# Causal gate taps as zero-padded 128-row matmuls, with a new order table

## The chip, the cores and the metric

One core of a Trainium2 chip. The metric is device time in microseconds; the kernel before took 230.55 us (median of three runs, 229.36 to 231.44).

## The reference

Two layers in a row: a linear attention with exponential features, and a gated unit with a causal convolution of five taps. Cut to what matters:

```python
# q, k, v: [8, 8, 576, 64] (batch, heads, sequence, head size); w_phi: [64, 128]
def phi(x):
    proj = x @ w_phi
    proj = proj - max(abs(proj), axis=-1)
    return concat(exp(proj), exp(-proj))              # 256 features
kv  = einsum('bhsf,bhsd->bhfd', phi(k), v)
den = phi(q) . sum_s(phi(k)) + 1e-6
x   = (phi(q) . kv) / den                             # [8, 576, 512], heads side by side

gate_pre[:, s] = sum over t of conv_w[t] * x[:, s + t - 4]   # five taps, zeros before the start
gate = sigmoid(gate_pre)
out  = (gate * (x @ w_val)) @ w_out                   # float32, [8, 576, 512]
```

## The kernel before

The eight batches are a software pipeline. Each batch goes through the same stages, and several batches are in work at once:

- **Loads.** Batch 0's k and q come as float32 on SP's queue (L506, L504) and are transposed on TensorE (`tp32`, L514). Later batches' q and k come through GpSimd's queue with a cast (`load`, L528); batch 1 is transposed on TensorE (`tp16`, L533, tasks `xk1.0` to `xk1.2` and `xq1.*`, copied out by `tc16`, L538 or L540), batches 2 to 7 by DMA transposes on SP's queue (`xpose`, L543). v comes on SP's queue (L509). A few one-element copies on GpSimd (`hold`, `holdx`, L488 and L491) make the loads behind them wait.
- **Features.** 18 column blocks of 128 rows per batch, in five units of 4, 4, 4, 4 and 2. For each unit: a projection (`kp`, `qm`, L555), the absolute maximum on VectorE (L562), and two exponentials on ScalarE, of the plus and of the minus sign (`kexp`, L572; `qexp`, L657 and L660). For q the maximum is subtracted in a second projection (`qp`, L642 and L649) that needs the maxima of all units (`mqt`, L631, and `mqr`, L634).
- **State.** `ek` (L581) makes scale factors from k's maxima, `vs` (L588, L589) scales v by them on GpSimd, into VT, in two groups of two; `st` (L598) multiplies features and scaled v, and `kv` (L606 or L610) copies the result out.
- **Attention out.** `num` (L670, L677), normalization on VectorE (`nrm`, L688 and L691), transposes (`xtp`, L699 and L703), copies (L711, L716) into the tile XT, and `halo` on GpSimd (L720, L721), which puts the last positions of one half ahead of the other.
- **Gate and out.** XT holds even positions in partitions 0 to 63 and odd ones in 64 to 127, 288 of each. A tap is a product with a diagonal matrix of the tap's weights. Where a pair of taps fills both halves, one 128-row matmul does two taps (GF, L732, eight per gate task). The fifth tap of each parity touches one half only: a 64x64 quarter of the array with the matrix GQ (L739, four per gate task). Four gate tasks per batch; then `tanh` (L743), `val` (L751), the product (`gv`, L757), `out` (L775), copies to OUTS (L608, L612) and stores (L797, L803). `c_gt` (L472, L475, L477) builds GF and GQ once, on GpSimd.

TensorE works in shapes, which the rows give as rows*columns: 128*128, 64*128 (projections, `st`, `val`), 128*64 (L732 and L677) and 64*64 (L739).

Nothing is scheduled by the compiler. `build` lists the tasks; the table `ORDER` gives their order, written out by hand as numbers, and each engine and each queue gets its instructions in that order and runs them in order. `FLEX` says which engine does the tasks that may go to two, `BANKS` which of the eight PSUM banks each group uses. `WARM` and the tasks `warm` add matmuls on a tile of ones (L481), whose result nobody reads.

Of the kernel before, what the change touches and what calls it, by code (L numbers as in the profile page):

```python
# [28 lines left out]
NW = 14  # L29
# [5 lines left out]
    "8:7:5 21:7:1 214:5:1 "  # L35
# [6 lines left out]
    "15 16 18 17 20 19 22 21 24 35 23 37 26 25 36 39 57 27 38 59 41 32 34 170 40 43 61 60 33 172 55 42 73 74 64 47 171 174 58 "  # L42
    "193 311 49 63 44 0 28 76 62 56 50 29 48 65 93 75 45 94 67 53 91 66 54 30 46 92 51 68 97 173 31 89 98 77 188 90 184 52 "
    "185 95 194 96 69 186 189 72 79 5 187 99 228 2 71 100 229 104 313 190 105 70 226 80 9 106 227 101 78 1 103 234 191 110 "
    "175 235 192 10 111 230 178 102 182 179 183 107 112 231 180 108 195 312 11 181 232 109 84 233 81 197 203 82 206 196 6 85 "
    "113 83 314 204 198 8 7 114 199 12 201 319 236 237 205 86 200 320 115 238 202 207 87 210 4 88 116 239 208 315 14 240 118 "
    "117 316 209 211 119 122 212 128 317 241 129 215 242 123 217 124 318 214 125 120 130 213 176 131 243 321 216 329 121 13 "
    "332 3 322 126 331 177 127 132 218 324 330 354 433 434 219 323 355 247 221 248 435 139 220 352 140 353 250 141 436 252 "
    "358 359 149 222 251 249 325 437 150 133 327 356 134 357 244 438 135 246 360 361 223 326 245 333 224 439 136 225 328 137 "
    "265 335 362 266 142 138 363 334 337 143 145 144 338 336 151 339 367 152 440 369 146 253 340 370 254 441 368 267 268 255 "  # L50
    "341 259 442 372 269 256 261 343 260 364 371 443 262 147 366 444 342 148 450 365 446 447 263 452 154 449 445 451 166 155 "
    "257 264 562 448 563 258 458 565 167 344 459 453 347 485 564 345 461 273 346 274 486 454 460 348 455 270 275 477 478 162 "
    "456 271 566 481 457 158 482 163 479 272 480 376 159 349 377 160 483 284 484 378 156 462 350 161 464 285 373 465 351 157 "
    "276 374 567 463 277 487 286 466 488 568 375 467 279 278 492 569 287 379 493 280 153 380 288 281 468 570 494 282 289 164 "
    "573 283 571 577 575 391 472 578 295 576 299 392 165 296 574 393 572 579 290 469 685 686 394 300 606 470 580 607 395 381 "
    "688 471 495 687 382 385 473 496 307 386 497 608 308 581 383 583 609 387 303 584 388 489 304 384 689 291 491 582 389 490 "
    "292 498 604 390 499 474 605 475 500 585 476 610 588 405 611 399 406 690 400 586 410 407 401 691 396 587 411 501 397 612 "
    "503 414 692 613 398 502 589 402 415 591 614 403 693 408 590 404 615 293 592 616 409 593 297 510 618 595 301 506 511 168 "
    "412 617 507 294 696 413 622 298 699 729 812 813 516 730 302 624 425 416 169 594 517 504 623 814 426 421 698 505 518 619 "
    "422 519 815 508 621 697 599 512 429 620 513 727 816 430 509 628 596 629 520 431 728 731 600 630 597 694 625 732 598 735 "  # L60
    "432 627 514 736 417 626 515 712 733 418 695 715 601 734 714 700 602 702 713 521 603 524 703 522 817 527 523 701 525 528 "
    "530 526 818 529 531 704 532 737 705 708 819 537 711 738 707 539 538 820 709 535 706 305 540 633 710 427 536 739 423 716 "
    "533 634 309 740 722 306 631 534 741 748 428 632 856 750 745 424 935 857 541 643 746 635 936 310 644 639 723 747 636 542 "
    "937 640 749 751 645 637 646 753 938 558 543 638 647 752 823 559 717 854 862 641 826 863 939 546 855 825 724 718 642 547 "
    "860 725 861 554 726 824 742 555 858 744 719 859 827 720 743 828 940 651 721 648 941 652 649 662 653 650 754 829 419 663 "
    "654 548 755 830 831 556 655 832 756 942 420 656 766 549 864 833 767 760 757 557 550 834 865 943 835 761 821 768 837 660 "
    "544 769 560 551 758 770 661 838 869 759 657 870 836 822 664 944 871 866 665 658 868 762 666 763 659 867 872 545 667 979 "
    "873 839 980 764 561 677 842 945 765 874 673 678 840 981 674 780 982 843 675 771 841 850 781 679 772 985 782 774 986 552 "
    "676 773 977 775 978 950 680 776 777 844 953 954 553 778 955 785 779 952 669 786 668 951 783 845 670 956 671 789 784 957 "
    "875 672 790 849 983 877 846 984 946 847 876 787 848 949 878 788 851 880 947 962 791 879 852 965 804 853 948 963 958 987 "  # L70
    "805 883 959 964 796 988 966 884 881 960 972 893 882 887 797 894 889 961 885 888 992 973 989 994 886 890 798 895 800 896 "
    "991 891 799 808 801 993 897 968 892 974 967 990 1001 975 1002 998 976 681 1003 809 999 969 682 810 995 1000 970 907 996 "
    "971 904 908 997 905 792 811 909 1004 906 1006 1005 793 1012 1007 1010 1016 1013 1008 916 1011 898 1009 1017 1014 901 917 "
    "1018 899 902 1019 910 1015 903 794 900 1020 806 914 683 911 795 912 802 807 1024 913 684 1021 915 803 1025 1027 1026 "
    "1030 1028 1031 1022 1029 923 1032 1037 924 1023 925 1033 1039 926 1034 1035 1040 1038 927 919 928 1036 931 929 920 1041 "
    "1054 932 918 921 930 1046 933 1055 922 1058 1056 1047 934 1042 1048 1059 1062 1057 1060 1050 1043 1049 1051 1044 1063 "
    "1052 1061 1045 1053 "
)
FLEX = (
    "ADAADAAAAAPPAPPDAAAADDAADAPPDPPDDAAADPPDPPDDADAPPAPPDAAAAAPPAPPDAADDPPAPPAAADADPPDPPDDADAPDDPPADDDDA"  # L80
)
BANKS = (
    "460006544445500124166757234523230145452301456767723672301674501445674652345230145234501276045505450101236723016701016767"
    "674230145670101011236736601674501014523236503323016723674501454567232370123456723450124567741230123236745236732374567452"
    "323450123452367010016767230167676452322367450167016767453636623674567452301452301454500101010101232320101732014501676767"
    "010122154523230145674545676767454450145674545450012303223672301010145236636423236745456701010145014524523670167452323457"
    "201230145450123457466234567014567230123674545701672301672345230177674501234545016744555"
# [69 lines left out]
def build(plan, em=None):  # L157
# [16 lines left out]

    for i in range(NW):
        A("warm", 0, i, "PE", 0.44, fn("warm2"), [], plan.group("warm", 1), 0)

    for b in range(B):
# [144 lines left out]
        for j in range(4):  # L323
            g = plan.group("gate", 2)
            ga = A("gate", b, j, "PE", 0.52, fn("gate", b, j, 0), xall, g, 2)
            gt = h["gate", b, j] = A("gate", b, j, "PE", 0.14, fn("gate", b, j, 1), [ga], g, 7, rank=-1)
            h["tanh", b, j] = A("tanh", b, j, "ACT", act(576), fn("tanh", b, j), [gt, G("gv", b - 1, j)], g)
# [25 lines left out]
class Emit:  # L353
    def __init__(self, nc, tc, ctx, q, k, v, w_phi, moe_w_val, moe_conv_w, moe_w_out, out):
# [63 lines left out]
        self.GQ = T("GQ", [P, H, D])  # L418
# [3 lines left out]
        for i in range(2):  # L422
            nc.gpsimd.memset(self.MQP[i][:, :], 0.0)
            nc.gpsimd.memset(self.XT[i][:, :, :, 0:HALO], 0.0)
# [41 lines left out]
    def c_gt(self, t):  # L466
        nc = self.nc

        for c, taps in ((0, (2, 3, 0, 1, 4)), (1, (3, 4, 1, 2, 0))):
            r = slice(c * D, (c + 1) * D)  # L470
            for i, tap in enumerate(taps):
                nc.gpsimd.tensor_copy(self.SC[r, :, i:i + 1], self.cwP[r, :, tap:tap + 1])  # L472
        with nc.allow_low_precision("bf16 taps"):
            for i in range(4):
                nc.gpsimd.tensor_tensor(self.GF[:, :, i, :], self.SC[:, :, i:i + 1].to_broadcast([P, H, D]),  # L475
                                        self.ID2[:, :].unsqueeze(1).to_broadcast([P, H, D]), ALU.mult)
            nc.gpsimd.tensor_tensor(self.GQ[:, :, :], self.SC[:, :, 4:5].to_broadcast([P, H, D]),  # L477
                                    self.ID2[:, :].unsqueeze(1).to_broadcast([P, H, D]), ALU.mult)
# [3 lines left out]

    def warm2(self, t):
        for _ in range(2):
            self.warm(t.grp.banks[0])
# [238 lines left out]
    def gate(self, t, b, j, part):  # L724
# [9 lines left out]
        else:  # L734
            for par, s, c in ((0, 0, 0), (1, 2, 1)):
                for h2 in range(2):
                    h = 2 * j + h2
                    rows = slice(c * D, (c + 1) * D)
                    self.nc.tensor.matmul(self.PS[h2 * D:(h2 + 1) * D, t.grp.banks[par], 0:R], self.GQ[rows, h, :],  # L739
                                          X[rows, h, :, HALO - 8 * s:HALO - 8 * s + XH], start=False, stop=True)  # L740
# [121 lines left out]
```

## Time and the profile before

| | |
|---|---|
| time, three runs | 230.55 us (229.36 to 231.44) |
| span of the profiled execution | 233.1 us |
| last matmul of the profiled execution | starts 225.76, busy 1.89 us for the last eight |
| TensorE busy | 211.9 us (91%), 4027 matmuls |
| ScalarE busy | 181.7 us (78%) |
| VectorE busy | 176.4 us (76%) |
| GpSimd busy | 103.0 us (44%) |
| DMA | 39.87 MB, mean 171 GB/s |

The profile is one execution, and matmuls are pipelined, so a busy TensorE is not a TensorE at its peak: the distance between the starts of two groups of matmuls tells more than their busy time. In a timeline row the first number is the start in us from the span's start, the second the busy time; a row ends with the number of instructions (x8) and, in brackets, the idle time before it and what ended it. In the chain of work that ended last, the columns are start, share of time in us, and what. In a row of windows, the columns are the window, its length, busy time of PE, PEld, DVE, ACT and POOL, the granted TensorE clock, the DMA share and GB/s.

### The profile page before, as it was taken

The page shows a single profiled execution, that of the slowest core. Times are in us where ns is not written, and L with a number is a line of the kernel's source. Part 1 is how long each engine was busy: PE and PEld are TensorE (multiplying, and loading weights), DVE is VectorE, ACT ScalarE, POOL GpSimd, SP SyncE. Part 2 cuts the span into 40 slices and gives each one's busy share as a digit, 9 for nine tenths or more (in the row PEclk, how much of TensorE's full clock was granted, in tenths as well). Part 3 has the DMA queues.
Part 4 walks back from the last instruction along what each step waited for, and adds up shares of the span by engine and source line. Part 5 has one row for each costly group of instructions (what it writes and reads, how often), then busy time and mean ns, then how long its engine had stood idle before and what let it go on. Part 6 is the DMA issues. An engine that isn't in the chain of part 4 may idle for free.

```text
span 233.1 us, 9168 instructions
## 1 busy us (share of the span) xinstructions
PE 211.9 (91%) x4027; PEld 145.5 (62%) x4027; DVE 176.4 (76%) x264; ACT 181.7 (78%) x267; POOL 103.0 (44%) x158
## 2 busy tenths in 40 slices
PE   7888997699998999999998599999999999999990
PEld 3566555567676576666766367676665867676640
DVE  2569776998789877998899549796888899583361
ACT  2878999799899987998898479978998999913320
POOL 2715992694059329800495006940009739100020
PEclk9999999999999999999999979999999999999999
DMA  6999935999699779968999981969984106156156
GB/s 199 338 257 272 208 55 160 209 181 174 116 207 242 127 160 178 302 114 114 229 167 296 167 232 30 148 126 229 263 277 143 52 3 139 37 83 204 45 177 184
DMA packets 49426, 39.87 MB, mean 171 GB/s; under 512 B 33706, under 2 KB 38826, under 8 KB 49322
## 3 DMA queue, kind: packets, MB, share of 16 engines
q1 hardware_dynamic: 43136, 29.63, 52.4%
q0 software_dynamic: 5760, 9.31, 23.8%
q8 instruction: 31, 0.51, 0.8%
q10 hardware_dynamic: 490, 0.35, 0.5%
q14 instruction: 9, 0.07, 0.1%
HBM read 30.49 MB, written 9.44 MB: 171 GB/s over the span
## 4 chain that ended last, share of the span: by engine, by line
PE 59%; DVE 16%; DMA 6%; POOL 5%; issue 5%; ACT 4%; ACTq 1%; SPq 1%; DVEq 0%
PE PS L751 12%; PE PS L775 10%; PE PS L732 7%; PE PS L555 7%; PE PS L598 6%; DVE MK L562 4%; DMA kT<-KQN 4%; DVE XN L691 4%; PE PS L670 3%; DVE MQP L562 3%; PE PS L739 3%; POOL VT L588 3%; PE PS L642 3%; DMA KTIL<-in_k_dram 2%; DVE GV L757 2%
## 5 line engine op out<-in xcount | busy, mean ns | idle before, releaser
L588 POOL TENSOR_TENSOR VT<-VN,EK 128x1152 bf16<-128x1152 f32 x31 | 65.9, 2125 | 66.5 <-ACT EK L581 55.5
L572 ACT ACTIVATE KTIL<-PS 128x1024 bf16<-128x1024 f32 (+1 forms) x80 | 72.4, 946 | 6.5 <-PE PS L555 4.3
L657 ACT ACTIVATE QTIL<-PS 128x1024 bf16<-128x1024 f32 x64 | 62.5, 1035 | 3.7 <-PE PS L649 3.3
L562 DVE TENSOR_REDUCE MQP<-PS 128x8 f32<-128x1024 f32 (+1 forms) x40 | 44.2, 1113 | 6.6 <-PE PS L555 5.5
L562 DVE TENSOR_REDUCE MK<-PS 128x8 f32<-128x1024 f32 (+1 forms) x40 | 43.9, 1111 | 4.4 <-PE PS L555 4.0
L751 PE MATMUL PS<-XT,WV 64*128 64x288 bf16 x512 | 35.5, 283 | 0.4 <-DVE XN L691 0.2
L757 DVE SCALAR_TENSOR_TENSOR GV<-TH,PS 128x576 bf16<-128x576 bf16 x32 | 23.7, 752 | 15.4 <-PE PS L751 10.5
L743 ACT ACTIVATE TH<-PS 128x576 bf16<-128x576 f32 x32 | 20.2, 654 | 16.6 <-PE PS L739 16.4
L775 PE MATMUL PS<-WOUT,GV 128*128 128x512 bf16 x128 | 31.7, 380 | 0.0
L751 PEld LDWEIGHTS <-WV 64*128 64x128 bf16 x512 | 24.8, 94 | 8.0 <-issue 2.4
L598 PE MATMUL PS<-VT,KTIL 64*128 64x65 bf16 x1152 | 24.5, 191 | 5.1 <-issue 3.5
L598 PEld LDWEIGHTS <-KTIL 64*128 64x128 bf16 x1152 | 21.4, 95 | 8.0 <-issue 5.2
L691 DVE TENSOR_TENSOR XN<-PS,RCP 128x512 bf16<-128x512 f32 x32 | 22.1, 692 | 1.1
L732 PE MATMUL PS<-XT,GF 128*64 128x288 bf16 x256 | 21.5, 301 | 0.3 <-DVE MQP L562 0.2
L670 PE MATMUL PS<-KV,QTIL 128*128 128x65 bf16 x512 | 20.1, 193 | 1.5 <-DVE GV L757 0.5
L670 PEld LDWEIGHTS <-QTIL 128*128 128x128 bf16 x512 | 18.2, 97 | 5.0 <-issue 2.7
L612 ACT ACTIVATE OUTS<-PS 128x512 f32<-128x512 f32 x22 | 13.3, 605 | 9.6 <-PE PS L775 9.1
L775 PEld LDWEIGHTS <-GV 128*128 128x128 bf16 x128 | 11.0, 97 | 11.6 <-issue 1.1
L720 POOL COPY XT<-XT 128x224 bf16<-128x224 bf16 x8 | 3.0, 375 | 34.2 <-DVE XT L716 22.3
L555 PE MATMUL PS<-W,kT 64*128 64x128 bf16 x288 | 15.4, 225 | 2.8 <-ACT kT L522 1.0
L732 PEld LDWEIGHTS <-GF 128*64 128x64 bf16 x256 | 13.2, 112 | 4.5 <-issue 2.0
L555 PE MATMUL PS<-W,qT 64*128 64x128 bf16 x288 | 15.1, 222 | 0.8 <-ACT TH L743 0.6
(76 smaller groups left out, 265.6 us busy)
## 6 DMA issues: line engine op xcount, KB each, us to landing
VN<-in_v_dram SPq DMA_DIRECT2D x8, 1152.0 KB, 6.9
out_dram<-OUTS SPq DMA_DIRECT2D x31, 256.0 KB, 3.2
KQN<-in_q_dram POOLq DMA_DIRECT2D x6, 576.0 KB, 6.8
KQN<-in_k_dram POOLq DMA_DIRECT2D x6, 576.0 KB, 8.0
KTIL<-in_k_dram SPq DMA_DIRECT2D x4, 288.0 KB, 4.1
KTIL<-in_q_dram SPq DMA_DIRECT2D x4, 256.0 KB, 4.2
out_dram<-OUTS SPq DMA_DIRECT2D x14, 64.0 KB, 2.8
QTIL<-in_q_dram POOLq DMA_DIRECT2D x1, 576.0 KB, 9.4
```

Of the source, the lines that this page charges most:

```text
L555: nc.tensor.matmul(self.PS[:, t.grp.banks[par], i * P:(i + 1) * P], X[rows, (c0 + i) * P:(c0 + i + 1) * P], self.W2[rows, :], start=True, ...
L562: self.nc.vector.tensor_reduce(o, self.two(t.grp, n * P).rearrange("p a (c f) -> p a c f", f=F), AX.X, ALU.max, apply_absolute_value=True)
L572: self.nc.scalar.activation(self.KTIL[b % 2][:, s, c0:c0 + n, :, :].rearrange("p c a f -> p a c f"), self.two(t.grp, n * P).rearrange("p a ...
L588: eng.tensor_tensor(self.VT[g][:, s, :, 0:D], self.VN[b % 2][:, NC * g:NC * g + NC, :], e.to_broadcast([P, NC, D]), ALU.mult)
L598: nc.tensor.matmul(self.PS[:, t.grp.banks[ab], (s * 2 + x) * E1:(s * 2 + x + 1) * E1], self.KTIL[b % 2][rows, s, J // 2, J % 2, :], self.V ...
L657: self.nc.scalar.activation(o, i, AF.Exp, scale=1.0 - 2.0 * s)
L670: nc.tensor.matmul(self.PS[:, t.grp.banks[h // 4], (h % 4) * E1:(h % 4 + 1) * E1], Q[:, s, c % 2, h, (c // 2) * P:(c // 2 + 1) * P], self. ...
L691: nc.vector.tensor_tensor(o.rearrange("p (g h) d -> p g h d", g=ng), n[:, :, :, 0:D], rc.unsqueeze(3).to_broadcast([P, ng, 4, D]), ALU.mult)
L732: self.nc.tensor.matmul(self.PS[h2 * D:(h2 + 1) * D, t.grp.banks[par], 0:R], self.GF[:, h, i, :], X[:, h, :, HALO - 8 * s:HALO - 8 * s + X ...
L751: nc.tensor.matmul(self.PS[:, t.grp.banks[par], 0:R], self.WV2[rows, h, j * P:(j + 1) * P], X[rows, h, :, HALO:XW], start=(h == 0), stop=( ...
L757: nc.vector.scalar_tensor_tensor(out=self.GV[b % 3][:, j, :, :], in0=self.TH[j][:, :, :], scalar=1.0, in1=self.two(t.grp, R), op0=ALU.add, ...
L775: nc.tensor.matmul(self.PS[:, t.grp.banks[0], :], lhsT, self.WOUT[:, j, :], start=(j == 0), stop=(j == 3))
```

## The change

The quarter matmuls of L739 become 128x64 matmuls: GQ gets one 64-column matrix per half, with zeros in the rows of the other half, and the matmul reads all 128 partitions of XT. Two memsets write the zeros. The task is planned in the shape of the other taps (mode 2) and with a planned length of 0.26 instead of 0.14. The 14 `warm` tasks go, `WARM` becomes one entry, and `ORDER`, `FLEX` and `BANKS` are new.

```diff
-NW = 14
...
 WARM = (
-    "8:7:5 21:7:1 214:5:1 "
+    "10:0:6 "
 )
...
 ORDER = (
-    "15 16 18 17 20 19 22 21 24 35 23 37 26 25 36 39 57 27 38 59 41 32 34 170 40 43 61 60 33 172 55 42 73 74 64 47 171 174 58 "
...
+    "0 1 2 3 4 6 8 21 23 25 10 11 5 7 9 20 156 12 43 22 45 46 14 18 13 47 50 19 15 44 59 62 61 26 158 16 17 160 297 27 28 29 "
...
-    for i in range(NW):
-        A("warm", 0, i, "PE", 0.44, fn("warm2"), [], plan.group("warm", 1), 0)
...
-            gt = h["gate", b, j] = A("gate", b, j, "PE", 0.14, fn("gate", b, j, 1), [ga], g, 7, rank=-1)
+            gt = h["gate", b, j] = A("gate", b, j, "PE", 0.26, fn("gate", b, j, 1), [ga], g, 2, rank=-1)
...
-        self.GQ = T("GQ", [P, H, D])
+        self.GQ = T("GQ", [P, H, 2, D])
...
             nc.gpsimd.memset(self.MQP[i][:, :], 0.0)
+            nc.gpsimd.memset(self.GQ[(1 - i) * D:(2 - i) * D, :, i, :], 0.0)
...
-            nc.gpsimd.tensor_tensor(self.GQ[:, :, :], self.SC[:, :, 4:5].to_broadcast([P, H, D]),
-                                    self.ID2[:, :].unsqueeze(1).to_broadcast([P, H, D]), ALU.mult)
+            for c in range(2):
+                r = slice(c * D, (c + 1) * D)
+                nc.gpsimd.tensor_tensor(self.GQ[r, :, c, :], self.SC[r, :, 4:5].to_broadcast([D, H, D]),
+                                        self.ID2[r, :].unsqueeze(1).to_broadcast([D, H, D]), ALU.mult)
...
-                    rows = slice(c * D, (c + 1) * D)
-                    self.nc.tensor.matmul(self.PS[h2 * D:(h2 + 1) * D, t.grp.banks[par], 0:R], self.GQ[rows, h, :],
-                                          X[rows, h, :, HALO - 8 * s:HALO - 8 * s + XH], start=False, stop=True)
+                    self.nc.tensor.matmul(self.PS[h2 * D:(h2 + 1) * D, t.grp.banks[par], 0:R], self.GQ[:, h, c, :],
+                                          X[:, h, :, HALO - 8 * s:HALO - 8 * s + XH], start=False, stop=True)
```

What the new numbers of `ORDER` mean at the start of the queues, by the built program (a task's unit stands behind the point; `t` marks transposes and their copies):

```
TensorE before: ... qm0.4 qm0.0 xq1.2t xq1.0t qm0.3 kp0.3 xq1.1t warm mqt0 qm1.1 warm qp0.1 ... xk1.0t xk1.2t ...
TensorE after:  ... tpQ3 c_cw tpQ1 xk1.2t qm0.3 qm0.4 xk1.0t qm0.2 kp1.4 kp1.1 xq1.0t qm0.0 qm0.1 xq1.2t xk1.1t xq1.1t mqt0 qp0.4 ...
ScalarE before: ... kexp0.3 kexp0.3 qexp0.1 qexp0.1 ek0.1 qexp0.0 qexp0.3 qexp0.0 xk1.2t qexp0.3 qexp0.2 ...
ScalarE after:  ... kexp0.2 kexp0.2 copyQ1 xk1.0t kexp1.4 kexp1.4 kexp1.1 kexp1.1 ek0.1 xq1.0t xk1.1t ek0.0 qexp0.4 ...
GpSimd before:  hold load(q1) load(k1) WV load(q2) EB vs0.0 load(k2) vs0.0 c_gt vs0.1 vs0.1 vs1.0 vs1.0 halo0 holdx WOUT vs1.1 ...
GpSimd after:   EB hold load(q1) load(k1) WV load(q2) load(k2) c_gt vs0.1 vs0.1 vs0.0 vs0.0 vs1.1 holdx WOUT load(q3) load(k3) vs1.1 halo0 vs1.0 vs1.0 ...
SP before:      ... v0 v1 v2 kT2 qT2 WVcopy kT3 ...
SP after:       ... v0 v1 kT2 qT2 WVcopy v2 kT3 ...
```

In the whole program, TensorE's shape changes 204 times from one task to the next before and 121 times after; the two parts of a gate task follow each other directly in 4 of 32 cases before and in 28 after.

## The prediction

> **What bounds the kernel now.** I read the page first (busy shares, chain), then TensorE's timeline for the price of a change of tile shape, then the timelines of ScalarE and GpSimd over the first 66 us, because the new order differs most there.
>
> ```profile
> span 233.1 us, 9168 instructions
> PE 211.9 (91%) x4027; PEld 145.5 (62%) x4027; DVE 176.4 (76%) x264; ACT 181.7 (78%) x267; POOL 103.0 (44%) x158
> ...
> PE 59%; DVE 16%; DMA 6%; POOL 5%; issue 5%; ACT 4%; ACTq 1%; SPq 1%; DVEq 0%
> ```
>
> TensorE holds most of the chain, but ScalarE is busy 78%: where batches start late, either can set the end. TensorE's timeline shows what a change of shape costs; the start of the next group shows when the array was free.
>
> ```profile
> 48.88 0.40 PE L555 MATMUL PS<-W,qT 64*128 64x128 bf16 x8
> 49.10 0.76 PE L598 MATMUL PS<-VT,KTIL 64*128 64x65 bf16 x36
> ...
> 50.56 0.68 PE L732 MATMUL PS<-XT,GF 128*64 128x288 bf16 x8
> 51.17 0.40 PE L555 MATMUL PS<-W,qT 64*128 64x128 bf16 x8
> 51.50 0.32 PE L739 MATMUL PS<-XT,GQ 64*64 64x288 bf16 x4
> 51.75 0.29 PE L642 MATMUL PS<-qT,W 64*128 64x256 bf16 x2
> ```
>
> Eight L555 matmuls hold the array 0.22 us when the next group has the same 64x128 shape (48.88 to 49.10) and 0.33 us when it has not (51.17 to 51.50): a change of shape costs 0.11 us. The chain gives the taps:
>
> ```profile
> 58.48 0.61 PE PS L732 x8
> ...
> 156.59 1.10 PE PS L732 x16
> ...
> 214.87 0.49 PE PS L739 x12
> ```
>
> Eight more L732 cost 1.10 - 0.61 = 0.49 us, 0.12 a pair. Four quarters cost 0.25 us alone (51.50 to 51.75) and twelve 0.49, so each further four cost 0.12: the four run side by side, and the rest of the 0.25 is the change of shape.
>
> These lines mark the start of each batch's numerators (`num`, L670 and L677), where all of a batch's exponentials must be done, and the one long gap:
>
> ```profile
> 39.12 0.65 PE L670 MATMUL PS<-KV,QTIL 128*128 128x65 bf16 x16 [0.25 <-DVE KV L606]
> 59.27 0.44 PE L677 MATMUL PS<-KV,QTT 128*64 128x65 bf16 x16
> 87.95 0.66 PE L670 MATMUL PS<-KV,QTIL 128*128 128x65 bf16 x16
> 113.42 1.15 PE L670 MATMUL PS<-KV,QTIL 128*128 128x65 bf16 x32
> 131.92 0.25 PE L598 MATMUL PS<-VT,KTIL 64*128 64x65 bf16 x5 [2.87 <-issue]
> ```
>
> With the prices above and the same method for the other lines (scores 0.44 us for ten matmuls, L598 0.58 for 36, L670 0.49 for 16, L751 0.98 for 16, L775 0.86 for 4), TensorE's queue of before holds 169.6 us of work from 39.1 to its end near 227.5: 151.1 of matmuls and 168 changes of shape. So 18.8 us are waits; 8.3 of them fall before 88 us and about 5 around the gap at 129, whose cause the profile does not show.
>
> **The change, part by part.**
>
> Taps. Per gate, four quarters (0.12 us) become two pairs of 128x64 (0.24 us): +0.12 x 32 gates = +3.9 us of TensorE. The number of matmuls and weight loads stays (128 and 128), and the loads (106 to 112 ns, L739 and L732) lie beside matmuls. When first and last taps follow each other one change of shape goes, 0.11 us, so a gate alone is neutral.
>
> The order. Counting shapes along both queues, 204 changes become 121; behind the first `num`, 168 become 105. 63 x 0.11 = -6.9 us. Three pairs of filler matmuls behind that point go (-1.3), and 0.6 us of other work is moved behind it. Sum from the first `num` on: 169.6 becomes 154.3 + 105 x 0.11 = 165.9, that is -3.7 us. By the Trainium skill, "TensorEngine Tiling (Array Packing)", Key Properties, a change of tiling mode drains the array, which would favour the change by its count of changes; its Performance Considerations speak against it, because a contraction of 64 rows is what two row tiles are for. The two rows above price both.
>
> Fillers. The 35 matmuls of L481 become 6. The 29 that go stood almost all before 48 us, where TensorE waits for others: worth nothing there, except for the clock (a rival below).
>
> GpSimd. Two memsets of GQ (512 elements; the 256-element L424 takes 0.31 us, so 0.3 to 0.7 each) and the EB copy (L442, 2.15 us), which moves to the front, fit into the 5.45 us in which GpSimd waits before 7.56. GQ's product becomes two of 64 partitions; the row for 128 partitions is 1.06 us, so +0 to +1.1. With the taps (1.50 + 4.11 + 2.1) it now stands ahead of the first VT, which waits for EK anyway until about 31; without that cover it would cost 1.1.
>
> The start. This is the part that I find dearest.
>
> ```profile
> 8.41 0.75 POOL L528 DMA_DIRECT2D QTIL<-in_k_dram  x1
> ...
> QTIL<-in_k_dram POOLq DMA_DIRECT2D x1, 576.0 KB, 17.5
> ...
> 22.70 1.94 ACT L657 ACTIVATE QTIL<-PS 128x1024 bf16<-128x1024 f32 x2 [0.61 <-PE PS L649]
> ```
>
> Batch 1's k lands at 8.41 + 17.5 = 25.9. Everything issued ahead of it on SP and GpSimd is unchanged (the next k load, which moves from 22.1 to about 10.5, stands behind it in GpSimd's queue), so I keep 25.9. Before, TensorE asked for it only at 26.7 and ran batch 0's queries first, so that ScalarE was exponentiating them from 22.7. After, the transpose `xk1.2` stands on TensorE ahead of `qm0.3`, and ScalarE's copy `xk1.0` ahead of all query exponentials. Behind `xk1.2` queue all of batch 0's query projections; VectorE's maxima wait for them, and ScalarE for `mqr0`. ScalarE has some 14 us of work from 5.5, so it is idle from about 19 to 27.2.
>
> Then, on ScalarE: copy 1.0, `kexp1.4` 1.1, `kexp1.1` 1.9, EK 0.35, copies 1.0 + 1.0, EK 0.35: 33.9. VectorE from 26.3: two small copies 0.3 each, four maxima at 1.14, two at 0.61, `mqr` 0.3: 33.0, the same time. Then `qexp0` and one half of `kexp1.0`: 1.2 + 9 x 0.93 = 9.6: 43.5. GpSimd's four VT (2.12 + 0.26 each) from the first EK at 31.2, then L598 and KV: 43.0. So the first `num` is near 43.8 instead of 39.1: +4.7.
>
> Next, EK of batch 1 comes after five more half exponentials, near 48.5. GpSimd: VT 50.9, then the hold, WOUT and two loads (0.2 + 0.8 + 0.6 + 0.8) 53.3, VT 55.7, halo 56.3, two VT 61.1. TensorE: `st1.0` 62.3. Its KV copy is now ScalarE's, behind `kexp2.3`: 65. `num1` is near 65.3 instead of 59.3: +6. To `num2`, ScalarE's list holds 28 us against TensorE's 25.6: 94.5 with 1 us of waits, +6.5. From `num2` to `num3` TensorE has 19.4 us (before 24.5, in 25.5 us elapsed) and ScalarE 19.3; with 1.9 of waits 115.8, that is +2.4. Of the shift, 4 us are won back, because less stands between these marks; but 106.5 us remain on TensorE behind `num3` against 104.5: +2.0. Sum +4.4.
>
> On the profiled execution that is 233.1 + 4.4 = 237.5, a factor of 1.019. That execution lies above the median of the three runs (230.55), perhaps by the gap at 129, which I leave in both. 230.55 x 1.019 = 235.
>
> Earlier transposes are a gain inside this sum: SP issued kT of batch 2 at 36.96 behind the third VN load, which waited for VT; now it stands ahead of that load and can go when its k has landed, near 33. The 0.98 us that TensorE waited for it at 45.1 goes; `kp2` is asked for later than that anyway. The third VN load goes behind both transposes and the WV copy, to about 42; its first user, a VT of batch 2, comes near 70, so its 6.9 us to landing are hidden (the cover gone, at most those 6.9).
>
> **The rivals.**
>
> TensorE alone decides (faster). If the late start is made up before `num3`, or batch 1's k lands by 21, TensorE's -3.7 us arrives: 230.55 - 3.7 = 226.8. For it: 59% of the chain, and waits of only some 5 us behind 88 us, the gap left out. Against it: 25.9 in the trace, and ScalarE's list. It decides if `num3` starts before 111.4 (113.4 - 2.0).
>
> The two cancel (within 1%; a measurement of this kernel can tell about 1% from no change). The first 4.7 is lost, but GpSimd's four VT of batch 1 cost no further 1.3 and `num2` is late by 3 or 4 instead of 6.5, since ScalarE's lists up to there (45.6 us by my prices) have a few instructions that another engine delays anyway: +1 or +2 at the end, 231 to 232.9.
>
> The clock (slower still). A gap of 2.87 us in TensorE was followed by a slow stretch:
>
> ```profile
> 132.00:156.00 24.00, 23.82 (x466) 16.33 (x467) 18.80 (x29) 19.08 (x29) 11.66 (x17) 0.93 0.74 136
> ```
>
> 0.93 of 24 us means 1.7 us lost, one stretch of 3.4 us at half rate. The new gap is some 8 us, and no fillers follow. If the half rate stays from 26 to 44, TensorE's 9.6 us there become up to 19 and set the pace with ScalarE: +1.7 to +5 on top, 237 to 240. The Trainium skill, "TensorE: Matmul & The Clock Gate", Why this matters for your kernels, says that gaps over about 3 us drop the clock; the row agrees.
>
> **How the numbers follow.** Forecast as worked out, 232.9 to 237: 0.45. TensorE alone: 0.16. Cancelled: 0.23. Clock: 0.16. Range 227.5 to 240.5: from just inside the first rival to the far end of the last. Faster by over 1%: 0.16; within 1%: 0.23; slower: 0.61.
>
> **What would show it.** Right: ScalarE idle some 8 us before a copy into kT near 27, `num0` near 44, `num1` near 65, `num3` two or three us late, and L739's successor at 0.24 us a gate. Wrong: `xk1` before 22, ScalarE busy between 19 and 27, or waits behind `num3` unlike those of before.

## The result and the profile after

The changed kernel takes 536.78 us (median of four runs, 536.02 to 542.96) against 229.96 for the kernel before (229.26 to 231.44): a ratio of 2.34 [2.324, 2.355]. The forecast was 235.0, with a range up to 240.5. Here and below a ratio compares undisturbed runs alone and a median takes all runs, so the two can differ a little.

The page of the kernel after: its span, its busy times, and the granted clock in 40 slices.

```profile
span 534.2 us, 9116 instructions
...
PE 299.0 (56%) x3998; PEld 204.7 (38%) x3998; DVE 180.8 (34%) x266; ACT 190.5 (36%) x265; POOL 104.2 (20%) x161
...
PEclk9556555565567557676557697685866675676999
```

VectorE and ScalarE are busy for 180.8 and 190.5 us, hardly more than before (176.4 and 181.7), in 2.3 times the span. The work has not grown; it is waiting. The loss has no single place either: every slice looks alike, and the clock is low almost throughout. Two groups of the same page (busy time and mean ns of one, then the idle time ahead of them and what ended most of it):

```profile
L651 ACT ACTIVATE QTIL<-PS 128x1024 bf16<-128x1024 f32 x64 | 63.5, 1027 | 87.6 <-PE PS L643 35.5
...
L744 PE MATMUL PS<-XT,WV 64*128 64x288 bf16 x512 | 54.3, 371 | 25.2 <-DVE MK L556 6.4
```

An exponential takes 1027 ns (before 1035), but 87.6 us of idle time stand ahead of the 64 of them (before 3.7). `val` on TensorE takes 371 ns where it took 283, along with a clock of 0.67 on the mean against 0.99. The low clock comes with the waits and does not cause them: runs below that take the waits away bring it back to 0.94 or 0.95 without one more filler.

The next view says whose wait it is. It is the timeline of ScalarE and VectorE, from the middle of the run:

```profile
148.76 0.76 DVE L750 SCALAR_TENSOR_TENSOR GV<-TH,PS 128x576 bf16<-128x576 bf16 x1 [1.47 <-PE PS L592]
...
149.60 1.02 ACT L566 ACTIVATE KTIL<-PS 128x1024 bf16<-128x1024 f32 x1 [7.37 <-DVE GV L750]
150.66 1.23 DVE L556 TENSOR_REDUCE MQP<-PS 128x8 f32<-128x1024 f32 x1 [1.15 <-ACT KTIL L566]
151.92 1.02 ACT L566 ACTIVATE KTIL<-PS 128x1024 bf16<-128x1024 f32 x1 [1.29 <-DVE MQP L556]
152.99 1.17 PE L592 MATMUL PS<-VT,KTIL 64*128 64x65 bf16 x36 [4.05 <-ACT KTIL L566]
...
158.88 1.02 ACT L566 ACTIVATE KTIL<-PS 128x1024 bf16<-128x1024 f32 x1 [0.70 <-PE PS L549]
159.94 1.22 DVE L556 TENSOR_REDUCE MQP<-PS 128x8 f32<-128x1024 f32 x1 [8.05 <-ACT KTIL L566]
161.19 1.02 ACT L566 ACTIVATE KTIL<-PS 128x1024 bf16<-128x1024 f32 x1 [1.29 <-DVE MQP L556]
```

The two engines take turns: in the lines from 149.60 to 151.92, and again at 159.94 and 161.19, each starts within 0.1 us of the other's end and names the other as its releaser. Yet nothing flows between these instructions. The exponential at 149.60 makes k's features of one unit of a batch, the maximum at 150.66 reads that batch's q projections, and the product `gv` at 148.76 works on an earlier batch. All of them only read PSUM, and in different banks: by the new table the exponential's group has banks 1 and 7, the maximum's 4 and 6, the product's 0 and 3.

What they have in common stands in a helper that the change doesn't touch:

```python
def two(self, g, n):
    a, b = g.banks
    return self.PS[:, a:b + 1:b - a, 0:n]
```

A group of two banks is read through one view whose step is the distance of its banks. Before, all 232 two-bank groups have neighbouring banks (63 in 0 and 1, 56 in 2 and 3, 61 in 4 and 5, 52 in 6 and 7), so that step is 1. The new `BANKS` has neighbours in 36 of 232; 57 pairs are two apart, 43 three, 26 four, 39 five, 12 six and 19 seven. If an access counts as the whole stretch from its first bank to its last, banks 1 and 7 cover 4 and 6, 0 and 3 overlap 1 to 7, and groups that share nothing must follow one another. Added up over the list of waits, ScalarE and VectorE waited for each other 10.2 us in 16 waits before and at least 282 us in 106 waits after. The two largest of after (engine and line, for whom, us in total, number, longest):

```profile
DVE MQP L556 <- ACT KTIL L566: 24.7, 9, 8.1
ACT KTIL L566 <- DVE GV L750: 23.3, 6, 7.5
```

Matched instruction by instruction with the bank table, 100 of these waits, 271 us in all, stand between two groups that have no bank in common and whose stretches overlap. In the kernel before no wait of the two engines is of this kind.

The Trainium skill, "PSUM — Partial Sum Buffer", in "PSUM bank collisions raise a hardware error", says that no two engines may be in the same partitions of one bank at once, readers included, and that semaphores have to see to it. In the trace readers do take turns, but their banks differ, so by that rule alone the turns shown would not be needed; the experiments decide whether it is the stretch.

### The profile page after: what moved, and what is told of

The parts are those of the page before. It is cut to its first block, busy times and chain, and to the rows that moved or that the text cites. A ratio compares the mean times of both kernels' runs of the same rounds, so it can differ in the third digit from the quotient of the medians.

```text
span 534.2 us, 9116 instructions
## 1 busy us (share of the span) xinstructions
PE 299.0 (56%) x3998; PEld 204.7 (38%) x3998; DVE 180.8 (34%) x266; ACT 190.5 (36%) x265; POOL 104.2 (20%) x161
## 3 DMA queue, kind: packets, MB, share of 16 engines
q0 software_dynamic: 5760, 9.31, 10.2%
## 5 line engine op out<-in xcount | busy, mean ns | idle before, releaser
L582 POOL TENSOR_TENSOR VT<-VN,EK 128x1152 bf16<-128x1152 f32 x31 | 65.8, 2124 | 191.3 <-ACT EK L575 183.9
L651 ACT ACTIVATE QTIL<-PS 128x1024 bf16<-128x1024 f32 x64 | 63.5, 1027 | 87.6 <-PE PS L643 35.5
L744 PE MATMUL PS<-XT,WV 64*128 64x288 bf16 x512 | 54.3, 371 | 25.2 <-DVE MK L556 6.4
L744 PEld LDWEIGHTS <-WV 64*128 64x128 bf16 x512 | 35.5, 120 | 39.4 <-issue 26.0
L768 PE MATMUL PS<-WOUT,GV 128*128 128x512 bf16 x128 | 43.6, 490 | 12.0 <-ACT KTIL L566 3.9
L726 PE MATMUL PS<-XT,GF 128*64 128x288 bf16 x256 | 32.2, 377 | 27.6 <-ACT TH L736 7.0
L592 PE MATMUL PS<-VT,KTIL 64*128 64x65 bf16 x1152 | 31.0, 222 | 27.5 <-DVE MK L556 12.5
L664 PE MATMUL PS<-KV,QTIL 128*128 128x65 bf16 x512 | 27.8, 221 | 26.5 <-ACT QTIL L651 9.6
L592 PEld LDWEIGHTS <-KTIL 64*128 64x128 bf16 x1152 | 28.5, 116 | 30.7 <-issue 16.7
L636 PE MATMUL PS<-qT,W 64*128 64x512 bf16 (+1 forms) x80 | 23.3, 515 | 26.8 <-ACT KTIL L566 10.0
L664 PEld LDWEIGHTS <-QTIL 128*128 128x128 bf16 x512 | 25.2, 116 | 31.7 <-issue 30.0
L549 PE MATMUL PS<-W,kT 64*128 64x128 bf16 x288 | 20.7, 263 | 27.2 <-ACT KTIL L566 11.9
L549 PEld LDWEIGHTS <-kT 64*128 64x128 bf16 x288 | 13.4, 114 | 34.4 <-issue 31.0
```

Source lines behind the costliest of these rows:

```text
L549: nc.tensor.matmul(self.PS[:, t.grp.banks[par], i * P:(i + 1) * P], X[rows, (c0 + i) * P:(c0 + i + 1) * P], self.W2[rows, :], start=True, ...
L582: eng.tensor_tensor(self.VT[g][:, s, :, 0:D], self.VN[b % 2][:, NC * g:NC * g + NC, :], e.to_broadcast([P, NC, D]), ALU.mult)
L592: nc.tensor.matmul(self.PS[:, t.grp.banks[ab], (s * 2 + x) * E1:(s * 2 + x + 1) * E1], self.KTIL[b % 2][rows, s, J // 2, J % 2, :], self.V ...
L651: self.nc.scalar.activation(o, i, AF.Exp, scale=1.0 - 2.0 * s)
L664: nc.tensor.matmul(self.PS[:, t.grp.banks[h // 4], (h % 4) * E1:(h % 4 + 1) * E1], Q[:, s, c % 2, h, (c // 2) * P:(c // 2 + 1) * P], self. ...
L744: nc.tensor.matmul(self.PS[:, t.grp.banks[par], 0:R], self.WV2[rows, h, j * P:(j + 1) * P], X[rows, h, :, HALO:XW], start=(h == 0), stop=( ...
```

## The experiments

Theory: the stretch between the two banks of a pair makes the waits, and nothing else in the change matters at this size. Rivals: the new order is bad by itself (it has the same queues whatever the banks); the padded taps make the waits; the new bank table has too little room between uses of a bank, whatever the pairs.

**Only the distance, in the kernel before.** The banks are renamed, one to one, so that order, taps and reuse of every bank stay. In the first, each pair is four apart, in the second two apart.

```diff
 # e3: banks 0 1 2 3 4 5 6 7 become 0 4 1 5 2 6 3 7
-    "460006544445500124166757234523230145..."
+    "230003622226600412433767152615150426..."
 # e7: banks 0 1 2 3 4 5 6 7 become 0 2 1 3 4 6 5 7
-    "460006544445500124166757234523230145..."
+    "450005644446600214255767134613130246..."
```

> The kernel before, its order, engines, taps and fillers kept, and only the banks renamed one for one: 0,1,2,3,4,5,6,7 become 0,4,1,5,2,6,3,7, so that each pair lies four banks apart and the same groups share the same two banks as before. Theory A: every pair's stretch now meets those of the others, so the time rises to 350 us or more, with ScalarE and VectorE taking turns. Rivals B, C and D (order, fillers, taps): nothing of theirs is changed, 229 to 232 us.

> The kernel before with the banks renamed one for one: 0,1,2,3,4,5,6,7 become 0,2,1,3,4,6,5,7. Pairs are two apart; the stretch 0 to 2 meets only the pair 1-3, and the stretch 4 to 6 only the pair 5-7. Theory A in its exact form (the tracked stretch runs from the first bank to the last): far less than the 634 us of pairs four apart, where each stretch meets all three others: 260 to 420 us. Its rival (any pair of banks that are not neighbours is tracked as all of the memory, or waits on everything): 550 to 680 us.

Four apart: 634.09 us, ratio 2.751 [2.736, 2.766]. Two apart: 350.86 us, ratio 1.521 [1.511, 1.531]. The page of the kernel four apart, and waits of the one two apart (engine and line, for whom, us in total, number, longest):

```profile
span 633.9 us, 9238 instructions
...
PE 368.7 (58%) x4027; PEld 220.6 (35%) x4027; DVE 183.4 (29%) x264; ACT 195.3 (31%) x267; POOL 103.5 (16%) x158
```

```profile
ACT KTIL L572 <- DVE MK L562: 9.4, 6, 3.9
DVE MK L562 <- ACT KTIL L572: 6.5, 6, 2.1
ACT KTIL L572 <- DVE GV L757: 6.3, 3, 2.3
```

A renaming alone makes the old kernel worse than the new one, with the same symptoms: the two engines wait for each other at least 299 us four apart and at least 101.6 us two apart. The step in the view alone is not what costs, since both have one; with pairs 0 and 2, 1 and 3 each pair overlaps one other, four apart each overlaps three others, and the cost (some 120 and 404 us) goes with that. Matched with the tables as above, 303 and 81 us of these waits stand between groups with no bank in common whose stretches overlap.

**The new bank table with split views.** Here the table stays scattered, but every instruction of ScalarE or VectorE on a two-bank view becomes two, each on one bank. The same edit in the kernel before is the control.

```diff
+    def one(self, g, a, n):
+        return self.PS[:, g.banks[a], 0:n]
...
-        self.nc.scalar.activation(self.TH[j][:, :, :], self.two(t.grp, R), AF.Tanh)
+        for a in range(2):
+            self.nc.scalar.activation(self.TH[j][:, a, :], self.one(t.grp, a, R), AF.Tanh)
...
 # likewise amax, kexp, kv, qexp, nrm, gv
```

> The changed kernel with its order and its scattered bank table kept; each instruction of ScalarE and VectorE that reads two banks (exponentials, maxima, tanh, gate product, KV copy, normalization) is split in two, one per bank. Theory A: the false waits go, 240 to 290 us (some 350 more instructions at 0.06 to 0.1 us each on the two engines). Rival E (the chip itself is slow when two far banks are used at once): still above 400, since the same banks are in use at the same time.

> The kernel before with its order and its neighbouring banks, and each two-bank instruction of ScalarE and VectorE split in two, as in e5_split_views. It is the control for the price of the split: e5 had 7.8 us more ScalarE time and 8.3 us more VectorE time than e1. Theory A: neighbouring banks have no false waits to lose, so the split can only cost: 232 to 240 us. If it were faster than before by over 1%, splitting itself would be a gain, and e5 would not show what the false waits cost.

With the views split the changed kernel takes 238.60 us (235.58 to 239.67), ratio 1.027 [1.020, 1.033]; the control 231.95, ratio 1.006 [1.002, 1.009]. Of the 134% that the change cost, 2.7 are left, with not one bank, order or tap altered. The page of the changed kernel with split views:

```profile
span 236.0 us, 9584 instructions
...
PE 208.0 (88%) x3998; PEld 154.0 (65%) x3998; DVE 184.0 (78%) x453; ACT 191.0 (81%) x446; POOL 105.0 (44%) x161
```

Waits of the two engines for each other: 3.9 us in 7. This settles the cause: with the same banks in the same order, the views alone make the 300 us come or go. It also rules out that the scattered banks leave too little room.

**Neighbouring pairs for the new order.** Two tables in place of the new one, both with neighbours only: one takes the pair that was left unused longest in the order, the other the pair that is expected to be free first.

```diff
 # e1
-    "014554507523671623014637012616273424601254646460..."
+    "010140145123676723452367674567452364567014545234..."
 # e8
-    "014554507523671623014637012616273424601254646460..."
+    "010140764423670123450145670167012300167230101016..."
```

> The changed kernel with its order, engines and taps kept, and only the bank table replaced: every two-bank group gets two neighbouring banks (0-1, 2-3, 4-5 or 6-7), as in the kernel before. Theory A (a view of two banks that are not neighbours is tracked as the whole stretch from the first bank to the last, so that groups in between wait for each other): time falls from 537 to 225 to 245 us, granted clock back to 0.95 or more. Rival B (the order itself, its late start and its queues, costs the 300 us): stays above 450. Rival C (the fillers that went let the clock drop to half, and this alone makes it slow): the clock stays near 0.67, time above 400.

> As e1_adjacent_banks (the changed kernel, its order, engines and taps; neighbouring banks for each pair), with the pair for each group taken not as the one that stands longest unused in the list, but as the one whose last reader should be done first by the durations of the profile. Theory A: e1's 252 us still held real waits, for banks that its table reused too early; here 229 to 238 us, like e5 less its split. If e1's 15 us over e5 are the order's own, 248 to 256.

The first takes 252.36 us (247.82 to 254.84), ratio 1.081 [1.074, 1.088], and so misses the 245 expected, though not the drop; the second 236.76 (236.09 to 236.89), ratio 1.026 [1.023, 1.029]. So with neighbours the choice of the pair is still worth some 5%, presumably because the longest unused pair in the order is not the one whose last reader is done first. The second, with 7.8 us of waits between ScalarE and VectorE, is the change as the prediction had pictured it, and the base of the next experiments.

**The taps alone, in the old order and in the new.** The kernel before with the padded taps (the diff above without the tables and `WARM`), and the kernel of 236.76 us with the quarters put back.

> The kernel before with its order, banks, engines and fillers, and only the taps changed (zero-padded 128x64 matmuls instead of 64x64 quarters). Theory A: the taps are not what made it slow; by the sum of the prediction +3.9 us for the pairs and -1.9 us for 17 changes between the shapes 128x64 and 64x64 that go: 230 to 233 us (ratio 1.00 to 1.015). Rival D (the padded taps or their operands are the cause): above 400.

> As e8_chosen_adjacent with one edit undone: the fifth taps are 64x64 quarters again, with the old GQ. Same order and banks. By the prices of the prediction, per gate with both parts side by side -0.12 us for the pairs and +0.11 us for the change of shape: within 1 us of e8. If the padded taps save the drain of the array in the new order, e8 is faster than this by 2 us or more; if padding costs, slower by 2 us or more.

In the old order the taps alone make 234.02 us, ratio 1.015 [1.011, 1.019], some 3.4 us: just past the 233 us expected, though at the end of the expected ratio (more on this below). In the new order quarters give 237.04, ratio 1.027 [1.024, 1.031], where the padded taps gave 1.026 [1.023, 1.029]: no difference. The old order has 4 of 32 gates in which padded first and last taps follow each other, the new one 28: where they do, the change of shape that goes may pay for the longer taps.

**Fillers in the gap at the start.** In the new order TensorE waits for batch 1's k from 17.0 to 23.1 us. Its clock is at half from 13.6 us on, so from before that wait: TensorE is busy only 1.5 of the 4.1 us ahead of the drop, with no gap over 1.2 us. Fourteen filler matmuls ahead of the wait:

```diff
-    "10:0:6 "
+    "10:0:6 67:2:14 "
```

> e8_chosen_adjacent with 14 matmuls on ones (6 us at half rate) put on TensorE ahead of the transposes of batch 1's k, where it waits from about 18 to 25 us. Nothing else is changed. If the half rate after that gap costs time by itself (the clock rival of the prediction): the full rate comes earlier and the time falls by 1 to 4 us, to 233 to 236. If ScalarE's idle time alone sets the start: within 1 us of e8's 236.8.

238.13 us (234.47 to 241.67), ratio 1.031 [1.025, 1.037]: no gain. In its trace the clock is at half from 13.7 to 20.6 us, full to 24.0, and at half again to 34.2, in place of half from 13.6 to 34.1. The fillers brought it up for 3.4 us, but what followed, short groups with waits between them, did not keep it, and the transpose that all wait for came no earlier. Whether a clock that is kept up all the way would gain is not shown.

**Batch 1's k later.** Fourteen tasks of batch 1's k (transposes, copies, projections, maxima, exponentials) go behind batch 0's second query exponential, nearer to where the kernel before has them; the banks are chosen anew in the same way.

```diff
-    "... 177 33 168 169 53 81 82 83 164 34 84 178 79 165 80 197 200 199 185 188 187 198 157 170 ..."
+    "... 177 33 53 81 82 83 34 84 178 79 80 157 170 ..."
...
-    "... 166 167 172 85 86 173 99 63 100 101 93 95 90 94 ... 70 186 96 ..."
+    "... 172 85 86 173 99 63 100 101 93 95 168 169 164 165 197 200 199 185 188 187 198 166 167 186 90 94 ... 70 96 ..."
```

> e8_chosen_adjacent with fourteen tasks moved: the transposes of batch 1's k, their copies, and the projections, maxima and exponentials of its units 1 and 4 go behind the second query exponential of batch 0, as the kernel before has it in kind. Banks chosen again in the same way. By the prediction's step on the start, ScalarE then works on batch 0's queries instead of waiting for 8 us, and the 4 to 6 us that e8 is above before go: 229 to 233 us. If the start was not what e8 lost: 236 to 238.

236.6 us (234.41 to 239.88), ratio 1.022 [1.016, 1.028], which can't be told from the 1.026 without the move: a miss. ScalarE, in the timeline of this kernel:

```profile
24.57 1.21 ACT L655 ACTIVATE QTT<-PS 128x256 bf16<-128x256 f32 x4 [4.05 <-PE PS L644]
...
39.33 1.94 ACT L652 ACTIVATE QTIL<-PS 128x1024 bf16<-128x1024 f32 x2 [2.45 <-PE PS L644]
```

The 7.29 us in which ScalarE waits for k (below) only become waits of 4.05 and 2.45 us for query projections. The first of these had to wait for VectorE's maxima, and the second falls in a stretch at half clock (30.0 to 43.6 us). The first normalization of batch 0 starts at 46.1 us, against 46.3 without the move. So moving those tasks as a block is not the remedy; that the late k costs nothing does not follow, because the rest of the order was made for the early place.

**A new order.** Two orders searched for the padded taps with neighbouring banks, of 127 and 128 changes of shape; in the second the search counted 2.9 us for each transposing DMA on SP's queue, which is about what most rows of the traces show. `FLEX` and the place of the six fillers are new too.

```diff
 # ORDER, its first entries: the changed kernel, e9, e13
 "0 1 2 3 4 6 8 21 23 25 10 11 5 7 9 20 156 ..."
 "0 1 2 3 10 11 4 6 43 44 8 21 23 25 5 46 7 ..."
 "0 1 2 3 10 11 43 4 6 8 21 23 45 25 5 12 7 ..."
```

> A version that is meant to beat both: e12's taps (padded) with neighbouring banks, and its order improved task by task with the durations and waits that the profiles show (a change of shape at 0.11 us, k of batch 1 at 25 us). 127 changes of shape on TensorE against 204 before and 121 in the changed kernel. If those durations and the rule that readers of one bank wait for each other are enough: 217 to 226 us. If something else bounds it: 229 or more.

> A second version that is meant to beat both: padded taps, neighbouring banks, 128 changes of shape. e9's profile showed GpSimd waiting 27.6 us for two loads of v that stood on SP's queue behind transposes that hold it 2.7 to 3.5 us each; here the order is improved with those transposes counted as 2.9 us of SP's queue and with transfers taking turns. If what e9 lost was these loads: 220 to 229 us. If an order made from such durations cannot do better than the one before: 230 or more.

The first is a miss, 244.47 us, ratio 1.059 [1.053, 1.064]. Its waits, and SP's queue, point to a reason:

```profile
POOL VT L583 <- DMA VN<-in_v_dram: 27.6, 2, 18.1
```

```profile
56.70 3.18 SPq L538 DMA_TRANSPOSE kT<-KQN  x1
59.99 3.33 SPq L538 DMA_TRANSPOSE qT<-KQN  x1
63.44 0.57 SPq L448 DMA_DIRECT2D WV<-WV  x1
64.11 2.71 SPq L504 DMA_DIRECT2D VN<-in_v_dram  x2
```

v's loads stand behind two transposes, and GpSimd waits 18.1 us for the first. With the queue priced in, the second order takes 228.67 us (226.52 to 231.35), ratio 0.9935 [0.990, 0.997]: the best version, if only by 0.65%. The two orders differ in more than v's loads, so what those alone cost is not shown.

```profile
span 224.7 us, 9117 instructions
...
PE 198.5 (88%) x3998; PEld 147.3 (66%) x3998; DVE 175.1 (78%) x267; ACT 178.9 (80%) x262; POOL 105.9 (47%) x163
```

TensorE is busy 198.5 us in place of 211.9. The fillers make up to 8.7 of these 13.4 us (35 were busy 11.4 us, the six left 2.7); the rest, some 5 us, is what the padded taps with fewer changes of shape can have lightened it by. Its idle time grows from 21 to 26 us, so most of this is lost in waits.

## Why the prediction was wrong

**The step that failed: the bank table, which had no price.** The prediction took the change as taps, order, fillers, GpSimd and start, and priced the order by counting shapes and by adding up each engine's list, as if ScalarE and VectorE were held only by data and by their own queues ("ScalarE's list holds 28 us against TensorE's 25.6"). `BANKS` stood in the diff's own description as new. None of the sum's terms, none of the rivals and no end of the range contained it: it stood at nothing, without a reason. What the runs showed in its place: the two engines hold each other up for at least 282 us, and the table's measured price is about 300 us (the changed kernel against itself with split views); the sum of all terms that were worked out was 4.4. The two lines of `two` with a step of `b - a`, beside a table whose pairs all were neighbours before and mostly are not after, would have shown where to look; the size of the loss no row of the trace of before could have given, because it has no pair that is not neighbouring.

**The rest of the sum** can be judged with that fault taken away, by the kernel with chosen neighbouring pairs: 236.76 us, against 235 forecast; the ratio of 1.026 makes it 5.3 to 6.6 us slower, against 4.4. Where the loss lies was only half right.

*The start* came at the times told; its cause is less sure. ScalarE and TensorE in that kernel:

```profile
17.35 0.61 ACT L516 CAST qT<-PS 128x512 bf16<-128x512 f32 x1
25.25 1.01 ACT L534 COPY kT<-PS 128x1024 bf16<-128x1024 bf16 x1 [7.29 <-PE PS L527]
```

```profile
23.10 0.39 PE L527 MATMUL PS<-ident,QTIL 128*128 128x128 bf16 x2 [6.10 <-DMA QTIL<-in_k_dram]
...
44.54 0.65 PE L664 MATMUL PS<-KV,QTIL 128*128 128x65 bf16 x16 [0.64 <-DVE KV L600]
...
64.35 0.45 PE L671 MATMUL PS<-KV,QTT 128*64 128x65 bf16 x16
```

ScalarE idles 7.29 us (told: some 8) before the copy into kT, at 25.25 (27.2); k itself landed at 23.1, 2.8 us sooner than the row of before said. `num0` starts at 44.54 (43.8), `num1` at 64.35 (65.3), `num2` at 92.03 (94.5). But where batch 1's k was moved and ScalarE's wait for it was gone, `num0` came no sooner; in the best order it did. The first `num` of those two kernels:

```profile
44.35 0.65 PE L665 MATMUL PS<-KV,QTIL 128*128 128x65 bf16 x16 [0.50 <-DVE KV L601]
```

```profile
38.81 0.65 PE L665 MATMUL PS<-KV,QTIL 128*128 128x65 bf16 x16 [1.05 <-DVE KV L601]
```

The best order has ScalarE at batch 0's queries from 21.73 us and the full clock up to 25 us. So the late start can be avoided, but the runs do not part the wait for k from the low clock and the order of the queries.

*From there to `num3`* the gain was larger than priced: `num3` starts at 112.96, where 115.8 was told and 113.42 stood before. From `num0` to `num3` 68.4 us pass instead of 74.3, so the late start is wholly made up there. But by the prediction's count 2.0 us more work stands behind this mark than before, so being level here is not yet a gain; the first rival ("TensorE alone decides") asked for 111.4.

*Behind `num3`* the prediction said "waits behind `num3` unlike those of before" would be wrong for it, and there they are. The control (the kernel before with split views; its trace lacks the gap at 129) and the kernel with chosen pairs, in windows:

```profile
115.00:138.00 23.00, 22.78 (x493) 16.37 (x490) 21.23 (x54) 22.09 (x52) 11.63 (x17) 1.00 1.07 214
138.00:150.00 12.00, 11.85 (x249) 8.33 (x246) 10.92 (x34) 11.24 (x26) 10.72 (x16) 1.00 0.87 181
150.00:162.00 12.00, 11.89 (x280) 8.34 (x274) 10.46 (x30) 10.46 (x25) 0.95 (x2) 1.00 0.89 173
```

```profile
115.00:138.00 23.00, 21.53 (x471) 16.37 (x471) 19.70 (x30) 20.36 (x30) 11.19 (x17) 1.00 1.03 263
138.00:150.00 12.00, 10.43 (x194) 7.66 (x190) 9.68 (x18) 9.59 (x14) 9.27 (x10) 1.00 0.92 125
150.00:162.00 12.00, 9.55 (x263) 7.29 (x260) 8.06 (x10) 9.46 (x16) 2.38 (x8) 1.00 0.84 209
```

TensorE is busy 46.5 of the 47 us from 115 to 162 in the control and 41.5 in the other. The chain of the latter names two of the releasers, and the same two waits stand, within 2 us of these places, in the chains of the kernel with split views and of the one with batch 1's k later:

```profile
116.14 7.80 DMA out_dram<-OUTS
124.06 0.70 DVE OUTS L602
...
139.85 5.85 DMA qT<-KQN
145.75 0.40 PE PS L549 x8
```

A copy into OUTS waits for a store that has not landed, and TensorE for a transpose that came behind another one, of kT, which held SP's queue for 7.53 us from 132.22. The control's chain has no DMA in this stretch; its transpose of kT took 5.96 us there, but began 5.6 us sooner. SP's queue was followed only up to 45 us in the prediction; behind that it was taken as unchanged. This part is read from the traces; no run took these two waits away one by one. TensorE's own idle time ahead of the two is 1.45 and 1.57 us; the rest of the 5 us is mainly two gaps of 1.32 and 1.07 us for which the profile names no releaser, like the one at 129 before, so their cause stays open, and they may belong to this execution alone.

*GpSimd* went as told: EB copy and memsets end before the hold, which waits 1.92 us for its DMA, and the GQ product takes 2.18 us in place of 1.06, the far end of the bound, ahead of 5.08 us of idle time.

*Taps and shapes.* The prices of single rows hold. Four padded taps take 0.24 us in the chain of the kernel with chosen pairs, as told, and 0.36 to 0.39 us in the old order where a change of shape stands with them, against 0.25 for the quarters. "A gate alone is neutral" fits the times in the new order, which quarters and padded taps leave the same. Sums of these prices fit the time less well. In the old order the padded taps also save 17 changes of shape (187 in place of 204), so the sum is 3.9 - 1.9 = +2.0 us; measured are 3.4 (2.5 to 4.3). In the new order the quarters need 170 changes in place of 121, so they would cost 49 x 0.11 - 3.9 = 1.5 us; measured are 0.3. The -6.9 us for 63 changes were not measured alone; the 5.9 us won between `num0` and `num3` contain them in part.

*The clock.* The half rate came, but sooner than that rival said: from 13.6 to 34.1 us, where the rival had 26 to 44 (granted 0.65 of full from 20 to 40 us). The 236.76 us lie just short of its 237. Fillers that shortened it by 3.4 us gained nothing, which speaks against the clock as the main cause, but no run kept it up all the way in this order.

## What to carry to other kernels

Look first at what a table of buffers does to the waits, before counting work: here renaming the banks of the old kernel, without touching an instruction's work, made it 2.75 times as long, more than the whole change did (2.34). Where one view spans two buffers, keep them neighbours, or use a view for each, which cost 0.6% here; and when two engines that share no data start at each other's ends all along a timeline, ask which stretch of memory each of them is taken to hold.

## What the runs showed of the hardware

- Readers of overlapping stretches of PSUM on ScalarE and VectorE are kept apart like a reader and a writer: 282 us of waits in the changed kernel, 3.9 with single-bank views. The releasers are semaphore events between the engines, and renaming or splitting moves them, so it is the built program that orders them and not a bank that is slow: the exponential takes 1027 ns as against 1035. Which part of the tools puts the semaphores in is not shown.
- Splitting ScalarE's instructions in two raised its busy time in the kernel before by 5% (181.7 to 191.3 us) and the time by 0.6%: successive ones overlap, 160 exponentials of 615 ns mean taking 79.2 us and not 98.
- A transposing DMA holds SP's queue 2.7 to 3.5 us in most rows, but one or two of the twelve of kT and qT in every other kernel take 4.9 to 8.3 us; the best order has none over 3.7. What makes them long was not tried.
- TensorE's clock is low where it has much idle time: 0.53 from 60 to 120 us of the changed kernel, where it is busy 32.5 of 60 us, and 1.00 in nearly all windows behind 40 us once the waits are gone. No long gap is needed: in the kernel with chosen pairs it halved at 13.6 us with no gap over 1.2 us in the 4.1 us ahead, of which TensorE was busy 1.5.
